# Three fused layers on one core: u's transfers grouped on the SP queue, the next y split in two portions, output products ahead of h2's last

## The chip, the cores and the metric

The kernel runs on one core of one Trainium2 chip. TensorE (PE) multiplies matrices, VectorE (DVE), ScalarE (ACT) and GpSimd (POOL) work element by element, SyncE's queue (SP) and ScalarE's issue DMA transfers. Each engine works through its own list in order, and semaphores hold an instruction until what it needs is there. The metric is the device time of the whole program in microseconds; lower is better.

## The reference

Three layers follow each other. The decay attention is linear, the next layer is `h - tanh(h)` between two products, the last a SoLU layer with a layer norm.

```python
for t in range(S):                    # S=768, 4 x 8 heads of 64
    state = gamma * state + einsum('bhd,bhe->bhde', k[:, :, t], v[:, :, t])
    y[:, :, t] = scale * einsum('bhd,bhde->bhe', q[:, :, t], state)
x = y.transpose(0, 2, 1, 3).reshape(3072, 512)
h = x @ w_in                          # 512 -> 2048
y = (h - tanh(h)) @ w_out             # 2048 -> 512
h2 = y @ w_in2                        # 512 -> 1024
sm = exp(h2 - max(h2)); sm = sm / (sum(sm) + 1e-9)
solu = h2 * sm
ln = (solu - mean(solu)) / sqrt(var(solu) + 1e-6) * g_ln
out = ln @ w_out2                     # 1024 -> 512
```

## The kernel before

Every factor of a product is held as two float32 parts, high and low (`xh`, `xl`), and a product is three matmuls: high by high, high by low, low by high. A matmul here is 128x128 weights against a 128x512 tile. The parts are made by a ScalarE cast (the high part) and a subtraction on VectorE or GpSimd (the low part).

The first product of the second layer, and h2 of the third, are done for a pair of token tiles together with seven products in place of eight (P1 to P7), whose operands are parts of y as they are (`yha`, `yla`, for P1, P2, P4) and sums of such parts (`ysum`, split into `yhs`, `yls`, for P5, P6, P7, P3). In a pair's h2 each product is six matmuls (L922), 42 in all. Some products are added up in a PSUM bank, others are copied by ScalarE (`keep2`, L929, tiles `part`) and added by VectorE (`add_half`, L937), which also takes the minimum of the negated row (`nm`). P6 continues in the bank of P1 and may start only when P1's copy has been taken; P7 continues P6's.

The 3072 tokens are 24 tiles, 12 pairs. The PE order of the last stage is written out by hand (`tc.manual_schedule`); the order on the other engines and on SP comes from a scheduler, which `pin` (`tc.keep_in_program_order`) binds to program order. Pair j's stage, `pair_of`, runs P1, P2, P6, P5, P7, P4, P3; behind it come the output products of pair j-1, `outs`, the odd tile and then the even one, each 24 matmuls into `po` (L986). Pair 0 lies inside the last slab of the layer before, whose steps f run from 0 to 15.

A tile of h2 becomes `u` in `soft`: exponential (L947, ACT), multiply with row sum (L949, DVE), subtract the mean (L951, ACT), sum of squares (L953, ACT), a 32x32 transposition (L955, DVE), then a store to DRAM, `ud` (L956, SP). `turn` loads it back with the token and feature axes exchanged (L969, SP), first the pair's odd tile, then its even one. `trans` splits it into `uh` (L160, ACT) and `ul` (L161, DVE). P4 finishes the odd tile, P3 the even one. `split_y` (L498 on ACT, L475 on POOL) and `sum_y` (L482 to L485, POOL) prepare y of later pairs; `load_y` (L468, SP) loads it. The store of y is L388, its copies out of PSUM are L385 (DVE) and L387 (ACT).

Of the kernel before, what the change touches and what calls it, by code (L numbers as in the profile page):

```python
# [26 lines left out]
F32 = mybir.dt.float32  # L27
F32R = mybir.dt.float32r
I32 = mybir.dt.int32
AF = mybir.ActivationFunctionType  # L30
ALU = mybir.AluOpType
# [5 lines left out]
P = 128  # L37
DM = H * D
# [7 lines left out]
NF1, NF2, NK = FF1 // P, FF2 // P, DM // P  # L46
# [42 lines left out]
def body(ctx: ExitStack, tc, z, w_in, w_out, w_in2, w_out2, g_ln, cst, tab, out):  # L89
    nc = tc.nc  # L90
# [8 lines left out]
    def pin(ins, on=True):  # L99

        if on:
            tc.keep_in_program_order(ins)

    def t4(shape, dtype, name):
        return big.tile(shape, dtype, tag="t4", name=name)

    def t2(shape, dtype, name):
        return mid.tile(shape, dtype, tag="t2", name=name)
# [10 lines left out]
    ud = [yd.tile([P, NF2 * P], F32, name=f"ud{i}") for i in range(NTT)]  # L119
# [37 lines left out]
    P1, P2, P6, P5, P7, P4, P3 = range(7)  # L157

    def parts(h, o, src, eng):
        nc.scalar.copy(h, src)  # L160
        eng.tensor_tensor(o, src, h.bitcast(F32), ALU.subtract)  # L161
# [297 lines left out]
    yl, ys, ysum = {}, {}, {}  # L459
# [11 lines left out]
    def on_pool(n, out, a, b, op):  # L471
        k = out.shape[1] // n
        for i in range(n):
            at = slice(i * k, (i + 1) * k)
            nc.gpsimd.tensor_tensor(out[:, at], a[:, at], b[:, at], op)  # L475

    def sum_y(j):
        t = yl[j]
        a11, a12, a21, a22 = (t[:, i, k : k + 2, :] for i in range(2) for k in (0, 2))
        s = ysum[j] = t4([P, 4, 2, P], F32, "ysum")  # L480
        s1, s2, s3, s4 = (s[:, i, :, :] for i in range(4))
        nc.gpsimd.tensor_tensor(s1, a21, a22, ALU.add)  # L482
        nc.gpsimd.tensor_tensor(s2, s1, a11, ALU.subtract)
        nc.gpsimd.tensor_tensor(s3, a11, a21, ALU.subtract)
        nc.gpsimd.tensor_tensor(s4, a12, s2, ALU.subtract)  # L485

    def split_y(j):
        t, s = yl.pop(j), ysum.pop(j)
        a22 = t[:, 1, 2:4, :]
        ya, ys_ = ([t4([P, 4, 2, P], F32R, f"y{n}{g}") for n in "hl"] for g in "as")  # L490
        flat = "p a k t -> p (a k t)"
        for to, lo, n, src in (
            (ya, 0, 2, t[:, 0, :, :].rearrange("p k t -> p (k t)")),
            (ya, 2, 1, a22.rearrange("p k t -> p (k t)")),
            (ys_, 0, 4, s.rearrange(flat)),
        ):
            h, o = (w[:, lo : lo + n, :, :].rearrange(flat) for w in to)
            nc.scalar.copy(h, src)  # L498
            on_pool(n, o, src, h.bitcast(F32), ALU.subtract)
        at = {P1: (ya, 0), P2: (ya, 1), P4: (ya, 2)}  # L500
        at |= {P5: (ys_, 0), P6: (ys_, 1), P7: (ys_, 2), P3: (ys_, 3)}
        ys[j] = {m: [w[:, i, :, :] for w in to] for m, (to, i) in at.items()}


    wl, xs, sums = {}, {}, {}
# [157 lines left out]
    for n in range(NF1):  # L663
# [8 lines left out]
        k = 2 * B + n - LATER  # L672
# [7 lines left out]
        else:  # L680

            dec1.n = 2 * NF1
            m = n - (NF1 - 4)
# [148 lines left out]
    for n in range(len(q) + 1):  # L832
        now, was = n < len(q), n > 0
        p, j = q[n] if now else (NSB, 0)
        todo = list(per[j]) if p == 1 else []
# [70 lines left out]

    w2p = ctx.enter_context(tc.tile_pool(name="w2p", bufs=7))
    sp = ctx.enter_context(tc.tile_pool(name="sp", bufs=3))
    uc, ut, sc2 = {}, {}, {}

    def bank2():
        pool, tag = bank_of[0]
# [29 lines left out]
    def soft(i, h, last):  # L942

        hn, nmx = h[0], h[1][last]
        ex = t4([P, FF2], F32, "ex")
        ssum = sp.tile([P, 1], F32, tag="ssum", name="ssum")
        nc.scalar.activation(ex, hn, AF.Exp, bias=nmx, scale=-1.0, accum_out=ssum)  # L947
        us = sp.tile([P, 1], F32, tag="us", name="us")
        nc.vector.scalar_tensor_tensor(ex, hn, 1.0, ex, ALU.mult, ALU.mult, accum_out=us)  # L949
        nc.vector.tensor_scalar(us, us, -1.0 / FF2, None, ALU.mult)  # L950
        nc.scalar.activation(hn, ex, AF.Identity, bias=us)  # L951
        ssq = sp.tile([P, 1], F32, tag="ssq", name="ssq")
        nc.scalar.activation(ex, ex, AF.Square, bias=us, accum_out=ssq)  # L953

        nc.vector.transpose(ex, hn)  # L955
        nc.sync.dma_start(out=ud[i], in_=ex)  # L956

        nc.vector.tensor_scalar(ssum, ssum, 1e-9, -1.0, ALU.add, ALU.mult)
        nc.vector.reciprocal(ssum, ssum)
        nc.vector.tensor_scalar(ssq, ssq, ssum, ssum, ALU.mult, ALU.mult)  # L960
        nc.vector.tensor_scalar(ssq, ssq, 1.0 / FF2, 1e-6, ALU.mult, ALU.add)
        sc = sp.tile([P, 1], F32, tag="sc", name="sc")
        nc.gpsimd.tensor_tensor(sc, ssq, mhalf, ALU.pow)
        nc.gpsimd.tensor_tensor(sc, sc, ssum, ALU.mult)
        uc[i], sc2[i] = hn, sc

    def turn(j):
        for i in (2 * j + 1, 2 * j):
            nc.sync.dma_start(  # L969
                out=uc[i].rearrange("p (c i b) -> p c i b", c=NF2, i=B),  # L970
                in_=ud[i].rearrange("(i a) (g c b) -> (a g) c i b", i=B, g=4, c=NF2),
            )

    def trans(i):
        u = uc.pop(i)
        uh, ul = (t4([P, NF2 * P], F32R, "u" + n) for n in "hl")
        parts(uh, ul, u, nc.vector)
        ut[i] = [w.rearrange("p (f t) -> p f t", f=NF2) for w in (uh, ul)]

    def outp(i):  # L980
        uh, ul = ut.pop(i)
        po = ps_o.tile([P, DM], F32, tag="o", name="po")
        for f in range(NF2):
            bh, bl = dec2.w[f]
            for n, (a, b) in enumerate(((uh, bh), (uh, bl), (ul, bh))):
                nc.tensor.matmul(  # L986
                    po, a[:, f, :], b, start=f == 0 and n == 0, stop=f == NF2 - 1 and n == 2
                )
        ob = t2([P, DM], F32, "ob")
        nc.scalar.activation(ob, po, AF.Copy, scale=sc2.pop(i))  # L990
        at = i % B * S + i // B * P
        nc.scalar.dma_start(out=out[at : at + P, :], in_=ob)
# [42 lines left out]
    for n, (s, f) in enumerate(steps):  # L1035
        if n:
            if f == 0:
                y_banks(s)
                if s == NSB - 1:
                    bank_of[:] = [(ps_a, "r"), (ps_a, "r"), (ps_h, "h"), (ps_h, "h")]  # L1040
            load_g(n + 5)
            load_wo(n + 4)
            if n + 2 < len(steps):
                split_p(n + 2)
            if n + 2 < NF1:
                split_wo(n + 2)
            products_y(f, gp.pop(n), wo[f], py)
        if f == NF1 - 1:
            keep_y(s, py)
        if s >= NSB - 3 and n % 2 == 0 and com.n[2] < 12:  # L1050
            com.step()
        m = n - 2 * NF1 - 6
        if m >= 0 and m % 3 == 0:
            step2(m // 3)
        if s == NSB - 1:
            if f == 0:
                load_y(0)
            if f == 2:
                sum_y(0)
                load_y(1)  # L1060
            if f == 5:
                split_y(0)
            if f == 9:
                sum_y(1)
                load_y(2)
            if f == 8:
                pair = Pair(0)
            for m in {8: (P1, P2), 9: (P6,), 10: (P5,), 11: (P7,), 12: (P4,), 13: (P3,)}.get(f, ()):
                pair.part(m)
            if f == 12:  # L1070
                split_y(1)
            if f == 13:
                turn(0)
            if f == 14:
                sum_y(2)
    G.close()
    M.close()

# [2 lines left out]
    ps_o = ctx.enter_context(tc.tile_pool(name="ps_o", bufs=2, space=PSUM, reuse_waits="tile"))  # L1081
    NJ = NTT // 2
# [3 lines left out]
    def pair_of(j, before):  # L1086
        pair = Pair(j)
        for n, m in enumerate((P1, P2, P6, P5, P7, P4, P3)):
            if n == 0 and j + 1 < NJ:
                split_y(j + 1)  # L1090
            if n == 2 and j + 2 < NJ:
                sum_y(j + 2)
            if n == 4 and j + 3 < NJ:
                load_y(j + 3)
            if n == 5 and before is not None:
                trans(2 * before + 1)
            pair.part(m)
        turn(j)
        if before is not None:
            trans(2 * before)  # L1100

    def outs(j, after=None):
        for half in (1, 0):
            outp(2 * j + half)
            if after is not None:
                trans(2 * after + half)

    with tc.manual_schedule(engines={mybir.EngineType.PE}):
        for j in range(1, NJ - 1):
            pair_of(j, j - 1)  # L1110
            if j < NJ - 2:
                outs(j - 1)
        pair_of(NJ - 1, None)
        outs(NJ - 3, NJ - 2)
        outs(NJ - 2, NJ - 1)
        outs(NJ - 1)


# [57 lines left out]
```

## Time and profile before

| | |
|---|---|
| median of 3 runs | 867.75 us (866.66 to 869.57) |
| profiled execution | 867.15 us, span 865.4 us |
| mean granted clock of PE | 0.986 of full speed |
| PE busy | 829.4 us, 96% of the span |
| PE weight load | 675.4 us, 78% |
| DVE busy | 540.7 us, 62% |
| ACT busy | 461.2 us, 53% |
| POOL busy | 291.6 us, 34% |
| last stage, pairs 1 to 11 | from 606.9 us to the span's end |

All in microseconds from the span's start. Busy times of engines overlap, so they don't add up. PE's busy share is near the whole, so the profile is read for the places where PE waits, and for the clock that was granted to it there. In a timeline, a row is a run of like instructions with its start and length; the square bracket is the idle time before it and what ended that.

### The profile page before, as it was taken

The page shows a single profiled execution, that of the slowest core. Times are in us where ns is not written, and L with a number is a line of the kernel's source. Part 1 is how long each engine was busy: PE and PEld are TensorE (multiplying, and loading weights), DVE is VectorE, ACT ScalarE, POOL GpSimd, SP SyncE. Part 2 cuts the span into 40 slices and gives each one's busy share as a digit, 9 for nine tenths or more (in the row PEclk, how much of TensorE's full clock was granted, in tenths as well). Part 3 has the DMA queues.
Part 4 walks back from the last instruction along what each step waited for, and adds up shares of the span by engine and source line. Part 5 has one row for each costly group of instructions (what it writes and reads, how often), then busy time and mean ns, then how long its engine had stood idle before and what let it go on. Part 6 is the DMA issues. An engine that isn't in the chain of part 4 may idle for free.

```text
span 865.4 us, 16366 instructions
## 1 busy us (share of the span) xinstructions
PE 829.4 (96%) x6296; PEld 675.4 (78%) x6296; DVE 540.7 (62%) x999; ACT 461.2 (53%) x868; POOL 291.6 (34%) x304
## 2 busy tenths in 40 slices
PE   5799999999999899999999999999899999999898
PEld 4678888788877687888788888888577777777786
DVE  3788975999858757223573979473555455555561
ACT  4655744646555546444462627244566666666662
POOL 4411100180634348433300350142544444444210
PEclk9899999999999899999999999999899999999999
DMA  9658654344899626955584647440766666665574
GB/s 361 254 215 301 254 190 156 120 147 177 303 362 335 236 82 223 411 198 174 195 337 127 226 121 281 148 169 25 171 145 147 147 147 145 146 147 122 121 162 105
DMA packets 168460, 169.41 MB, mean 196 GB/s; under 512 B 105664, under 2 KB 117952, under 8 KB 168384
## 3 DMA queue, kind: packets, MB, share of 16 engines
q1 hardware_dynamic: 160032, 153.38, 57.1%
q10 hardware_dynamic: 8352, 15.00, 4.7%
q8 instruction: 49, 0.80, 0.4%
q14 instruction: 27, 0.22, 0.1%
HBM read 107.02 MB, written 61.34 MB: 195 GB/s over the span
## 4 chain that ended last, share of the span: by engine, by line
PE 81%; DVE 5%; DMA 4%; ACT 3%; issue 3%; POOL 2%; SPq 0%; ACTq 0%; POOLq 0%; DVEq 0%
PE py L377 29%; PE ph L750 15%; PE po L986 14%; PE ph L922 11%; PE ph L352 8%; PE out L228 2%; DMA hn<-ud 2%; PE sc L228 2%; DMA z<-z 1%; DMA raw<-w_in 1%; ACT part L929 1%; POOL hs L768 1%; DVE hn L937 1%; POOL yls L475 1%; ACT uh L160 0%
## 5 line engine op out<-in xcount | busy, mean ns | idle before, releaser
L377 PE MATMUL py<-gp,w 128*128 128x512 f32 x768 | 175.4, 389 | 0.0
L377 PEld LDWEIGHTS py<-gp,w 128*128 128x128 f32 x768 | 144.1, 188 | 29.9
L986 PE MATMUL po<-w,uh 128*128 128x512 f32 x384 | 118.6, 390 | 0.0
L768 POOL TENSOR_TENSOR hs<-hs,th 128x512 f32<-128x512 f32 x48 | 66.8, 1395 | 95.8 <-ACT th L766 91.1
L986 PEld LDWEIGHTS po<-w,uh 128*128 128x128 f32 x384 | 72.1, 188 | 14.8
L352 PE MATMUL ph<-xh,w 128*128 128x512 f32 x256 | 82.1, 395 | 0.8 <-DVE w L154 0.8
L377 PE MATMUL py<-gh,w 128*128 128x512 f32 x256 | 79.2, 390 | 0.3 <-ACT gh L365 0.3
L986 PE MATMUL po<-w,ul 128*128 128x512 f32 x192 | 76.4, 398 | 0.6 <-DVE us L950 0.6
L153 ACT CAST w<-wf 128x512 fp32r<-128x512 f32 x70 | 43.1, 621 | 57.6 <-DVE wf L144 47.1
L922 PE MATMUL ph<-w,yhs 128*128 128x512 f32 x192 | 63.9, 416 | 6.4 <-ACT part L929 5.8
L475 POOL TENSOR_TENSOR yla<-yl,yha 128x256 fp32r<-128x256 f32 x36 | 26.3, 756 | 127.2 <-ACT yha L498 127.2
L766 ACT ACTIVATE th<-hs 128x512 f32<-128x512 f32 x48 | 30.3, 631 | 60.4 <-DVE hs L776 52.4
L937 DVE CUSTOM_DVE_ANT_0 hn<-ph,part 128x512 f32<-128x512 f32 x24 | 16.6, 691 | 72.5 <-ACT part L929 54.9
L154 DVE TENSOR_TENSOR w<-wf,w 128x512 fp32r<-128x512 f32 x70 | 51.2, 736 | 15.3 <-ACT w L153 14.5
L161 DVE TENSOR_TENSOR gp<-g,gp 128x512 fp32r<-128x512 f32 x64 | 48.4, 770 | 18.8 <-ACT gp L160 18.6
L750 PE MATMUL ph<-xh,wch 128*128 128x512 f32 x140 | 57.3, 409 | 1.6 <-DVE hs L776 1.6
L352 PEld LDWEIGHTS ph<-xh,w 128*128 128x128 f32 x256 | 48.0, 188 | 11.8 <-DVE w L154 1.3
L377 PEld LDWEIGHTS py<-gh,w 128*128 128x128 f32 x256 | 48.0, 188 | 10.6 <-ACT gh L365 0.7
L929 ACT COPY part<-ph 128x512 f32<-128x512 f32 x36 | 21.1, 586 | 64.7 <-PE ph L922 64.7
L750 PE MATMUL ph<-xh,wcl 128*128 128x512 f32 x140 | 55.4, 396 | 0.0
L750 PE MATMUL ph<-xl,wch 128*128 128x512 f32 x140 | 55.3, 395 | 0.0
L776 DVE TENSOR_TENSOR hs<-ph,part 128x512 f32<-128x512 f32 x48 | 32.9, 686 | 35.2 <-PE ph L750 20.8
(123 smaller groups left out, 1811.9 us busy)
## 6 DMA issues: line engine op xcount, KB each, us to landing
z<-z SPq DMA_DIRECT2D x48, 512.0 KB, 6.4
g<-gd SPq DMA_DIRECT2D x64, 256.0 KB, 5.3
raw<-w_in SPq DMA_DIRECT2D x24, 512.0 KB, 6.3
raw<-w_out SPq DMA_DIRECT2D x24, 512.0 KB, 4.4
gd<-hs SPq DMA_DIRECT2D x48, 256.0 KB, 3.9
ud<-ex SPq DMA_DIRECT2D x24, 512.0 KB, 4.5
hn<-ud SPq DMA_DIRECT2D x24, 512.0 KB, 5.8
y1d<-ysb SPq DMA_DIRECT2D x24, 256.0 KB, 3.9
```

The source lines that it names most:

```text
L153: pin(nc.scalar.copy(hi, wf), fixed)
L154: pin(eng.tensor_tensor(lo, wf, hi.bitcast(F32), ALU.subtract), fixed)
L161: eng.tensor_tensor(o, src, h.bitcast(F32), ALU.subtract)
L228: pin(nc.tensor.matmul(o, a, b, start=True, stop=True, skip_group_check=True), held[0])
L352: nc.tensor.matmul(ph, a[:, k, :], x, start=n == 0, stop=n == 3 * NK - 1), s < 2
L377: nc.tensor.matmul(py[e], a[:, cols], x, start=f == 0 and n == 0, stop=f == NF1 - 1 and n == 2)
L475: nc.gpsimd.tensor_tensor(out[:, at], a[:, at], b[:, at], op)
L750: nc.tensor.matmul(ph, a, x, start=first and n == 0, stop=n == 5, skip_group_check=True)
L768: eng.tensor_tensor(g, h, th, ALU.subtract)
L776: nc.vector.tensor_tensor(h, ph, part, ALU.add)
L922: nc.tensor.matmul(ph, x[:, r, :], w, start=first and n == 0, stop=n == 5, skip_group_check=True)
L986: nc.tensor.matmul(po, a[:, f, :], b, start=f == 0 and n == 0, stop=f == NF2 - 1 and n == 2)
```

## The change

Three things change, all in or near the last stage.

First, the store of `u` and its load are pinned, so on SP a pair's two stores come first and then its two loads.

Second, `split_y` can do one half: the direct parts (`yha`, `yla`) or the sums' parts (`yhs`, `yls`). In a pair, the direct half of the next pair's y is split after P1 and the sums' half after P6; the sums of the pair after that are taken after P7. In the last slab, `split_y(0)` moves from f=5 to f=4, `sum_y(1)` from 9 to 6, `split_y(1)` from 12 to 9, `sum_y(2)` from 14 to 11.

Third, the first three output products of the odd tile of the pair before (two with `uh`, one with `ul`) stand between P4 and P3 of pairs 1 to 10; the other 21 follow P3 as before.

```diff
-    def split_y(j):
+    def split_y(j, halves=(0, 1)):
...
+        for g in halves:
+            y = [t4([P, 4, 2, P], F32R, f"y{n}{'as'[g]}") for n in "hl"]
+            if g:
+                todo = ((0, 4, ysum.pop(j).rearrange(flat)),)
+                at = {P5: 0, P6: 1, P7: 2, P3: 3}
+            else:
+                t = yl[j]
+                todo = (
+                    (0, 2, t[:, 0, :, :].rearrange("p k t -> p (k t)")),
+                    (2, 1, t[:, 1, 2:4, :].rearrange("p k t -> p (k t)")),
+                )
+                at = {P1: 0, P2: 1, P4: 2}
+            for lo, n, src in todo:
+                h, o = (w[:, lo : lo + n, :, :].rearrange(flat) for w in y)
+                nc.scalar.copy(h, src)
+                on_pool(n, o, src, h.bitcast(F32), ALU.subtract)
...
-        nc.sync.dma_start(out=ud[i], in_=ex)
+        pin(nc.sync.dma_start(out=ud[i], in_=ex))
...
-            nc.sync.dma_start(
+            pin(nc.sync.dma_start(
...
-    def outp(i):
-        uh, ul = ut.pop(i)
-        po = ps_o.tile([P, DM], F32, tag="o", name="po")
-        for f in range(NF2):
+    def outp(i, fs):
+        uh, ul = ut[i]
+        if fs[0] == 0:
+            po_of[i] = ps_o.tile([P, DM], F32, tag="o", name="po")
+        po = po_of[i]
+        for f in fs:
...
-            if f == 5:
+            if f == 4:
                 split_y(0)
+            if f == 6:
+                sum_y(1)
             if f == 9:
-                sum_y(1)
                 load_y(2)
...
-            if f == 12:
+            if f == 9:
                 split_y(1)
+            if f == 11:
+                sum_y(2)
             if f == 13:
                 turn(0)
-            if f == 14:
-                sum_y(2)
...
         for n, m in enumerate((P1, P2, P6, P5, P7, P4, P3)):
-            if n == 0 and j + 1 < NJ:
-                split_y(j + 1)
-            if n == 2 and j + 2 < NJ:
+            if n == 5 and before is not None:
+                trans(2 * before + 1)
+            if m == P3 and before is not None:
+                outp(2 * before + 1, range(1))
+            pair.part(m)
+            if n in (0, 2) and j + 1 < NJ:
+                split_y(j + 1, (n // 2,))
+            if n == 4 and j + 2 < NJ:
                 sum_y(j + 2)
             if n == 4 and j + 3 < NJ:
                 load_y(j + 3)
-            if n == 5 and before is not None:
-                trans(2 * before + 1)
-            pair.part(m)
```

PE, from P4 of a steady pair (bank `ph2_7576`) to the second group of output products; P3 is what goes on in the bank of P5 and reads `yhs`, `yls`; `uh_7572` and `ul_7573` are the odd tile of the pair before. Before:

```order
L922 MATMUL ph2_7576<-w_6212,yha_7325 128x512 x2
L922 MATMUL ph2_7576<-w_6212,yla_7326 128x512
L922 MATMUL ph2_7554<-w_6069,yhs_7327 128x512 x2
L922 MATMUL ph2_7554<-w_6069,yls_7328 128x512
L922 MATMUL ph2_7554<-w_6249,yhs_7327 128x512 x2
L922 MATMUL ph2_7554<-w_6249,yls_7328 128x512
L986 MATMUL po_7633<-w2_6325,uh_7572 128x512 x2
L986 MATMUL po_7633<-w2_6325,ul_7573 128x512
L986 MATMUL po_7633<-w2_6388,uh_7572 128x512 x2
```

and changed (the lines of the file have shifted by 3 to 8):

```order
L925 MATMUL ph2_7576<-w_6212,yha_7334 128x512 x2
L925 MATMUL ph2_7576<-w_6212,yla_7335 128x512
L991 MATMUL po_7602<-w2_6325,uh_7572 128x512 x2
L991 MATMUL po_7602<-w2_6325,ul_7573 128x512
L925 MATMUL ph2_7549<-w_6069,yhs_7357 128x512 x2
L925 MATMUL ph2_7549<-w_6069,yls_7358 128x512
L925 MATMUL ph2_7549<-w_6249,yhs_7357 128x512 x2
L925 MATMUL ph2_7549<-w_6249,yls_7358 128x512
L991 MATMUL po_7602<-w2_6388,uh_7572 128x512 x2
```

The group of `w2_6325`, with its `ul` product, has moved ahead of P3's six products.

VectorE at the same place: `hn_7504` is the odd tile of this pair's h2 (its first row adds P7's `part`, the third takes P4's bank `ph2_7576`), `hn_7507` the even tile, which P3 finishes. Before:

```order
L937 ISA hn_7504,nm_7506<-ph2_7554,part_7569 128x512
L937 ISA nm_7506 128x1
L937 ISA hn_7504,nm_7505<-ph2_7576,part_7569,nm_7506 128x512
L937 ISA nm_7505 128x1
L161 TENSOR_TENSOR ul_7573<-hn_7319,uh_7572 128x1024
L937 ISA hn_7507,nm_7509<-ph2_7554,part_7552,nm_7508 128x512
```

and changed:

```order
L940 ISA hn_7504,nm_7506<-ph2_7549,part_7562 128x512
L940 ISA nm_7506 128x1
L940 ISA hn_7504,nm_7505<-ph2_7576,part_7562,nm_7506 128x512
L940 ISA nm_7505 128x1
L161 TENSOR_TENSOR ul_7573<-hn_7319,uh_7572 128x1024
L952 SCALAR_TENSOR_TENSOR ex_7584,us_7587<-hn_7504,ex_7584 128x1024
```

The subtraction that makes `ul_7573` stands behind the add of P4's bank in both; the multiply of the odd tile now comes ahead of the even tile's last add.

ScalarE around the beginning of pair 1: `ysb` are the copies of the last y, `hn` in L951 (changed: L954) and `ex` in L953 (changed: L956) belong to pair 0's tiles, `part` is the copy after P1. Before:

```order
L387 COPY ysb_6924<-py_6467 128x512
L387 COPY ysb_6930<-py_6469 128x512
L951 ACTIVATE hn_6684<-ex_6871,us_6874 128x1024
L953 ACTIVATE ex_6871,ssq_6878<-ex_6871,us_6874 128x1024
L498 CAST yhs_6957<-ysum_6907 128x1024
L929 COPY part_6976<-ph2_6969 128x512
```

and changed:

```order
L387 COPY ysb_6924<-py_6467 128x512
L954 ACTIVATE hn_6689<-ex_6876,us_6879 128x1024
L387 COPY ysb_6930<-py_6469 128x512
L956 ACTIVATE ex_6876,ssq_6883<-ex_6876,us_6879 128x1024
L932 COPY part_6962<-ph2_6955 128x512
L503 CAST yhs_6987<-ysum_6808 128x1024
```

The cast of the sums has moved behind the part copy, and one pass over the even tile has moved between the two copies of y.

## Rows read from the trace of the kernel before

**Rows 1.** Chain of waits, 634 to 656 us: start, length, what.
```profile
634.73 6.82 PE ph L922 x30
...
641.56 0.60 ACT part L929
...
642.18 0.69 DVE hn L937
...
642.94 1.66 PE ph L922 x6
```

**Rows 2.** Window of a steady pair: length, busy (count) by engine, PEclk, DMA, GB/s.
```profile
644.60:665.57 20.97, 20.92 (x91) 16.74 (x91) 11.01 (x27) 13.64 (x21) 9.23 (x15) 1.00 0.66 150
```

**Rows 3.** Timeline of PE, pair 1: start, length, work, idle before and releaser.
```profile
606.93 0.73 PE L922 MATMUL ph<-w,yha 128*128 128x512 f32 x2 [0.52 <-ACT ysb L387]
...
613.35 1.22 PE L922 MATMUL ph<-w,yhs 128*128 128x512 f32 x2 [3.41 <-ACT part L929]
...
620.27 0.62 PE L922 MATMUL ph<-w,yha 128*128 128x512 f32 x2
```

**Rows 4.** Timeline of ACT, pair 1.
```profile
611.77 1.04 ACT L498 CAST yhs<-ysum 128x1024 fp32r<-128x1024 f32 x1 [2.28 <-POOL ysum L485]
```

**Rows 5.** Timeline of ACT and PE, pair 11.
```profile
817.92 1.04 ACT L160 CAST uh<-hn 128x1024 fp32r<-128x1024 f32 x1 [1.16 <-DMA hn<-ud]
...
819.50 0.72 PE L922 MATMUL ph<-w,yhs 128*128 128x512 f32 x2 [2.35 <-ACT part L929]
...
823.95 0.39 PE L922 MATMUL ph<-w,yhs 128*128 128x512 f32 x1
```

**Rows 6.** Timeline of PE, an even tile's first `ul` product.
```profile
778.17 0.50 PE L986 MATMUL po<-w,ul 128*128 128x512 f32 x1 [0.41 <-DVE us L950]
```

**Rows 7.** Timeline of PE, pair 2.
```profile
634.56 0.62 PE L922 MATMUL ph<-w,yha 128*128 128x512 f32 x2
...
641.36 0.62 PE L922 MATMUL ph<-w,yha 128*128 128x512 f32 x2
...
644.98 0.50 PE L986 MATMUL po<-w,ul 128*128 128x512 f32 x1
645.32 0.62 PE L986 MATMUL po<-w,uh 128*128 128x512 f32 x2
```

**Rows 8.** Timeline of DVE, pair 2.
```profile
643.03 0.75 DVE L937 CUSTOM_DVE_ANT_0 hn<-ph,part,nm 128x512 f32<-128x512 f32 x1
...
643.70 1.22 DVE L161 TENSOR_TENSOR ul<-hn,uh 128x1024 fp32r<-128x1024 f32 x1
```

**Rows 9.** Timeline of ACT, pair 2.
```profile
642.04 1.05 ACT L160 CAST uh<-hn 128x1024 fp32r<-128x1024 f32 x1
```

**Rows 10.** Groups by line, 623 to 812 us: busy, mean ns, idle before.
```profile
L949 DVE SCALAR_TENSOR_TENSOR ex<-hn,ex 128x1024 f32<-128x1024 f32 x18 | 22.0, 1223 | 0.0
...
L947 ACT ACTIVATE ex<-hn,nm 128x1024 f32<-128x1024 f32 x18 | 20.8, 1154 | 12.3 <-DVE nm L937 12.3
```

**Rows 11.** Timeline of SP: a store of pair 0, an even load.
```profile
608.94 0.59 SPq L956 DMA_DIRECT2D ud<-ex  x1
...
662.55 0.59 SPq L969 DMA_DIRECT2D hn<-ud  x1
```

**Rows 12.** DMA issues on the page: count, size, median us from issue to landing.
```profile
ud<-ex SPq DMA_DIRECT2D x24, 512.0 KB, 4.5
hn<-ud SPq DMA_DIRECT2D x24, 512.0 KB, 5.8
```

**Rows 13.** Timelines of DVE and POOL: like subtractions, alone and beside GpSimd's.
```profile
594.08 0.69 DVE L161 TENSOR_TENSOR gp<-g,gp 128x512 fp32r<-128x512 f32 x1
...
602.18 1.89 POOL L475 TENSOR_TENSOR yls<-ysum,yhs 128x256 fp32r<-128x256 f32 x2
...
602.33 1.15 DVE L161 TENSOR_TENSOR gp<-g,gp 128x512 fp32r<-128x512 f32 x1 [0.56 <-ACT gp L160]
```

**Rows 14.** Window with a long PE wait in the second layer; columns as in rows 2.
```profile
335.50:339.00 3.50, 1.87 (x9) 1.49 (x9) 3.50 (x4) 0.63 (x1) 3.23 (x2) 1.00 1.02 381
```

## What was predicted

> **What bounds the kernel now.** I read the last stage first, since every edit lies there, and began with the chain of waits over one pair [rows 1]: it is TensorE nearly throughout, broken only by a ScalarE copy and a VectorE add after P7. The window from one pair's first output product to the next pair's [rows 2] says the same: 20.97 us, of which PE is busy 20.92. A pair issues 42 h2 and 48 output products. By the chain, 30 products take 6.82 us, so one goes out every 0.2273 us and ninety need 20.46. A steady pair therefore loses only about 0.5 us. The page's PE share, 96%, is an average; what can be won here is the sum of a few gaps, and what can be lost is any new gap on PE.
>
> The timelines show four gaps. I call them A to D.
> - A, start of pair 1 [rows 3, 4]: P1 waits 0.52 for ScalarE's copy of the last y, and P6 waits 3.41 because ScalarE's part copy stands behind the `yhs` cast at 611.77, which waited 2.28 for GpSimd's sums. Then the 18 products from 613.35 to 620.27 take 6.92 in place of 4.09: 2.8 more, at the lower of the clock's two levels (2.4 and 1.2 GHz).
> - B, every pair: P3 waits for VectorE's first add, then the first `ul` product waits for VectorE. Together this is the 0.5 us above.
> - C, pair 11 [rows 5]: P6 waits 2.35 for a part copy behind the `uh` cast at 817.92, which waited 1.16 for a load. The 12 products from 819.50 to 823.95 take 4.45 in place of 2.73: 1.72 more, in the same way.
> - D, even tiles: the first `ul` product waits for VectorE in six pairs, each 0.06 to 0.70 by the products' issue times, 1.8 together; the row of the worst is [rows 6].
>
> **The change part by part.** I count from the issue of P4's first product in pair 2, 641.36, as zero [rows 7]. No instruction's work changes; only places do.
>
> *Three output products before P3.* Before, P4 goes out from 0 to 1.36, P3 to about 3.0 (six products of 0.227, after a wait of 0.22), two `uh` products at 3.07, the `ul` product at 3.62 (644.98), and the next at 3.96 (645.32). The `ul` product waits for VectorE's subtraction, which runs 643.70 to 644.92, that is +2.34 to +3.56 [rows 8]. It comes there because ScalarE casts `uh` from 642.04 to 643.09 [rows 9], behind the part copy, and VectorE does the a1 add, then the a0 add of P4's result (643.03 to 643.78), then the subtraction. The order of VectorE and ScalarE there is the same in both programs. The a0 add must wait for P4, which has not moved, so `ul` is still ready at +3.56. What ran under that wait was P3, 1.36 us. Now P3 stands behind the `ul` product: PE issues P4 to 1.36, waits some 0.4 for `uh`, issues two products, waits some 1.4 for `ul`, issues it at +3.62, and only at +3.96 comes to P3, which ends at +5.32. Before, all these products were out at +3.96. The cost is P3's whole 1.36 us. Pairs 2 to 10 do this: 9 x 1.36 = +12.2. The gap B is in that: the stall for the a1 add goes, the wait for `ul` swallows it.
>
> *The even tile and the SP order (D).* After P3 come 21 odd products (4.77), so the even tile starts at +10.1 and its `ul` is needed at +10.5. P3's last add ends near 6.3 (0.75 long [rows 8]); the exponential of 1.15 and the cast of 1.05 behind it end near 8.7, the multiply of 1.22 near 8.9, the subtraction of 1.22 near 10.2 [rows 8 to 10]. So 0.3 us are spare, if the load has come. Before, the even load went out at 662.55, +21.2, behind the even store [rows 11]; now both stores go first, and I estimate the even load at +20, when the even store, issued near +14.7, has landed (4.5) and SP has come back. With 5.8 for the load [rows 12] it is there at +26, and the pair lasts 22.3, so it comes 4 us into the next pair, well before the cast at 7.7. The odd load now leaves near +15 in place of +13.7, lands at +21, and is needed at +23. D's 1.8 us go: -1.8. If the 0.3 us spare are not there, each pair pays what is missing; that is in the rivals.
>
> The Trainium skill, SBUF — State Buffer, section "SBUF: two separate sides", says that VectorE (with two inputs in SBUF) and GpSimd (reading SBUF) exclude each other from a shared port pair, and the second to come is blocked for the whole instruction. The trace agrees in kind [rows 13]: a 128x512 subtraction on VectorE took 0.69 alone and 1.15 beside GpSimd's. By that rule the even subtraction would be late whenever GpSimd's `yla` chain began ahead of it; the price is among the rivals.
>
> *The two portions of y (A).* `ysum` of pair 1 is now summed at step f=6 and cast after P6, so P6 no longer waits for GpSimd: 3.4 and the clock's part go. But two things are late in their place. ScalarE's order now has one 128x1024 pass (L954, 1.15 like [rows 10]) between the two copies of y, so P1 starts near 608.05 and not 606.93. And pair 1 too has the three products before P3: their `uh` needs tile 1's load. The store left at 608.94 [rows 11] and can now leave up to 0.8 earlier, since two of y's stores stand ahead of it on SP and not three; it lands 4.5 later, the load takes 5.8 [rows 12], the cast 1.05: `uh` at 619.5 to 620.3. PE, from 608.05 with 36 products (8.18), is through P4 at 616.2 and waits 3.3 to 4.1. From `uh` at 619.5 the `ul` is ready 1.25 later (the subtraction), at 620.8; one `ul` product, P3, 21 odd products and 24 even ones take 0.2 + 1.4 + 4.8 + 5.5, and the even `ul`, whose load comes after the odd one, costs perhaps 0.5: pair 1 ends near 633.2 at full clock. Before, it ended at 634.56, where pair 2's P1 begins [rows 7]. Stalls of 2.35 and 3.41 were followed by the lower clock [rows 3, 5]; I add C's 1.72 and get 634.9, a net +0.3; between -1.4 (no lower clock) and +1.8.
>
> *End (C).* ScalarE's order before pair 11 now has the even cast, the odd square, then the part copy of P1, and that cast waits for the exponential after P3 of pair 10, not for a load. The cast ends at 8.7, square and copy take 1.5 more: P6 at +10.25, where PE, with P1 and P2 (2.73) after +5.32, is ready at +8.05: 2.2 in place of 2.35, with another 0.2 at P7, and the same clock. Net +0.1. If all of C went it would be -4.1 (2.35 and 1.72).
>
> *Steps moved in the last slab.* GpSimd and ScalarE have gaps there and PE does not wait for them in the profile; 0, from -0.3 to +0.5.
>
> Sum: +12.2 - 1.8 + 0.3 + 0.1 = +10.8. The profiled execution took 867.15 (span 865.4), the median of three 867.75: 878.0 against the first, 878.6 by the second. I say 878.
>
> **The rivals.**
> 1. *ScalarE's part copies come free (not slower).* If the copies of pairs 1 and 11 no longer stand behind a cast that waits, A's whole 0.5 + 3.4 + 2.8 (waits and clock) and C's 4.1 go: about -10.8, with D -12.6, against +12.2: 866.8. The point from which it decides is a cost per pair of 1.40; under it the kernel is faster. For it: the y sums are early now. Against: the order puts L954 ahead of the second y copy, pair 1's new products wait for a load that lands near 618.5, and the cast ahead of pair 11's copy waits for P3. 8%.
> 2. *The clock falls in each pair.* The new waits, 0.4 and 1.4, have two products between them. A stretch of 3.50 us in which PE was busy 1.87, its idle time in one piece of 1.6, kept a granted clock of 1.00 [rows 14]; a wait of 2.35 was followed by the lower level [rows 5]. If each pair falls, 9 x 1.72 more: 893.5; if a third do, 883. 12%.
> 3. *The even tile is late.* GpSimd's `yla` subtractions now follow P1 and begin just after VectorE's even subtraction. Beside one, VectorE's subtraction took 1.15 in place of 0.69 [rows 13]; two of GpSimd's took 1.89, 0.95 each. One that goes first costs 0.95 less the spare 0.3, 0.65 in nine pairs, +5.9: 884; in half of them, 881. Against: the `yla` cast stands behind two ScalarE passes that come with or after the even tile's own cast. 12%.
> 4. *PE's wait is hidden*, because `ul` is ready at P4's end. Then B's 0.5 go too in ten pairs, with D: about 860. It needs the subtraction ahead of the a0 add, and the order has it behind. 3%.
>
> **How the numbers follow.** My own case has 65%: 878, with 874 to 881 for the terms of A and C and a tenth per pair either way. The range 871 to 888 takes in rival 3, the milder form of rival 2 and most of C's gain; it leaves out rivals 1 and 4 and the full form of 2. About 0.3% (2.6 us) is what a measurement of this kernel can tell. Faster by more: rival 4 and a little of 1, 0.05; within: the rest of 1, 0.06; slower: 0.89.
>
> **What would show it.** Right: in a pair of the changed kernel, two `uh` products after P4, then a wait of about 1.4 for VectorE at the `ul` product, P3 1.36 later than its old place, a period near 22.3; no wait at an even tile's `ul`; no wait for a part copy at pair 1's P6, but one of 2.5 to 4 after its P4. Wrong: a period under 21.3, a granted clock under 1.00 inside pairs 2 to 10, or VectorE's subtraction ahead of the a0 add.

## The result and the profile after

| | before | changed |
|---|---|---|
| median, the runs of one chip | 867.2 us (864.3 to 869.57, 4 runs) | 877.41 us (877.04 to 879.79, 4 runs) |
| ratio to before | | 1.0125, 95% interval 1.0089 to 1.0161 |
| profiled execution, span | 867.15, 865.4 us | 877.57, 875.7 us |
| PE busy | 829.4 us, 96% | 827.2 us, 94% |

The change made the kernel slower by 1.25%, 10.2 us between the medians and 10.3 between the spans. PE's busy time did not grow; its waiting did.

The timeline of PE in pair 2 answers to [rows 7]; P4 begins at 642.65. The columns are start, length, work, idle time before it and what ended that.

```profile
642.65 0.62 PE L925 MATMUL ph<-w,yha 128*128 128x512 f32 x2
...
644.43 0.73 PE L991 MATMUL po<-w,uh 128*128 128x512 f32 x2 [0.26 <-ACT uh L160]
646.27 0.50 PE L991 MATMUL po<-w,ul 128*128 128x512 f32 x1 [1.10 <-DVE ul L161]
646.60 0.62 PE L925 MATMUL ph<-w,yhs 128*128 128x512 f32 x2
```

The `ul` product goes out 3.62 after P4's first product, and the next thing 3.95 after it: just as before. But that next thing is now P3. VectorE in the same pair, answering to [rows 8]:

```profile
644.32 0.75 DVE L940 CUSTOM_DVE_ANT_0 hn<-ph,part,nm 128x512 f32<-128x512 f32 x1
...
644.99 1.22 DVE L161 TENSOR_TENSOR ul<-hn,uh 128x1024 fp32r<-128x1024 f32 x1
```

The subtraction runs from +2.34 to +3.56 after P4's first product, to the hundredth where it was. The groups by line from 623 to 812 us, in which eight pairs' early products lie, show what that sums to (busy, mean ns, idle before and releaser):

```profile
L991 PE MATMUL po<-w,uh 128*128 128x512 f32 x279 | 87.4, 394 | 2.1 <-ACT uh L160 2.1
L991 PE MATMUL po<-w,ul 128*128 128x512 f32 x139 | 55.3, 398 | 9.0 <-DVE ul L161 8.8 <-DVE ssq L964 0.3
```

Windows of the changed kernel, with the columns of [rows 2]: a steady pair, the stretch behind pair 1's wait, and pair 11's first products.

```profile
642.64:664.98 22.34, 20.98 (x91) 16.73 (x90) 11.13 (x26) 13.74 (x20) 9.13 (x16) 1.00 0.59 134
620.00:624.40 4.40, 4.35 (x9) 2.98 (x10) 2.64 (x6) 2.26 (x3) 0.00 (x0) 0.50 0.95 169
829.00:834.50 5.50, 3.48 (x15) 2.31 (x13) 4.98 (x12) 5.39 (x8) 0.74 (x2) 1.00 0.17 71
```

A pair lasts 22.34 in place of 20.97, at a granted clock of 1.00. The second window is at the lower level, the third is not. PE at the beginnings of pairs 1, 2 and 11 (answering to [rows 3, 5, 7]):

```profile
607.65 0.73 PE L925 MATMUL ph<-w,yha 128*128 128x512 f32 x2 [1.45 <-ACT ysb L387]
...
620.01 1.22 PE L991 MATMUL po<-w,uh 128*128 128x512 f32 x2 [3.90 <-ACT uh L160]
...
635.85 0.62 PE L925 MATMUL ph<-w,yha 128*128 128x512 f32 x2
...
831.58 0.73 PE L925 MATMUL ph<-w,yhs 128*128 128x512 f32 x2 [2.02 <-ACT part L932]
```

Pair 1's P6 waits for no copy any more; the 3.90 after its P4 stands in that place. The pair starts 0.72 later and ends 1.29 later than before (635.85 against 634.56): term A is +1.29. From there to pair 11's first product are 190.83 against 179.70 us, +11.13, of which 0.68 are three products that were issued behind it before: pairs 2 to 10 cost +10.45. From pair 11 to the end the kernel gains 2.12, less those 0.68: -1.44. Together 10.3, the difference of the spans.

SP's two stores and two loads of pair 2, now in that order (compare [rows 11]), and then the landing times of all loads of u in this kernel:

```profile
654.05 3.66 SPq L959 DMA_DIRECT2D ud<-ex  x2
658.88 4.26 SPq L972 DMA_DIRECT2D hn<-ud  x2
```

```profile
DMA to landing us min/median/max: 6.2/7.2/9.1
```

The odd load leaves at +16.2, and the median load takes 7.2 where [rows 12] had 5.8; both will matter below.

### The profile page after: what moved, and what is told of

Same layout as the page of the kernel before. It is cut to its first block, busy times and chain, and to the rows that moved or that the text cites. A ratio compares the mean times of both kernels' runs of the same rounds, so it can differ in the third digit from the quotient of the medians.

```text
span 875.7 us, 16359 instructions
## 1 busy us (share of the span) xinstructions
PE 827.2 (94%) x6296; PEld 674.0 (77%) x6296; DVE 542.4 (62%) x999; ACT 463.2 (53%) x868; POOL 291.3 (33%) x304
## 4 chain that ended last, share of the span: by engine, by line
PE 78%; DMA 7%; DVE 6%; issue 4%; ACT 4%; POOL 1%; SPq 0%; ACTq 0%; DVEq 0%; POOLq 0%
PE py L377 28%; PE ph L753 15%; PE po L991 12%; PE ph L925 9%; PE ph L352 9%; DMA hn<-ud 2%; PE out L228 2%; PE sc L228 2%; DMA raw<-w_in 1%; DVE ul L161 1%; DMA z<-z 1%; DVE hn L940 1%; DMA wcd<-wch 1%; DMA ud<-ex 1%; ACT part L932 1%
## 5 line engine op out<-in xcount | busy, mean ns | idle before, releaser
L991 PE MATMUL po<-w,uh 128*128 128x512 f32 x384 | 120.4, 395 | 6.3 <-ACT uh L160 6.3
L991 PEld LDWEIGHTS po<-w,uh 128*128 128x128 f32 x384 | 71.9, 189 | 24.9 <-ACT uh L160 10.5
L991 PE MATMUL po<-w,ul 128*128 128x512 f32 x192 | 76.6, 399 | 10.4 <-DVE ul L161 10.1
L475 POOL TENSOR_TENSOR yla<-yl,yha 128x256 fp32r<-128x256 f32 x36 | 28.6, 822 | 105.0 <-ACT yha L503 90.6
L925 PE MATMUL ph<-w,yhs 128*128 128x512 f32 x192 | 60.5, 397 | 2.1 <-ACT part L932 2.0
L160 ACT CAST gp<-g 128x512 fp32r<-128x512 f32 x64 | 38.7, 619 | 29.8 <-DMA g<-gd 17.7
```

The source lines that it names most:

```text
L925: nc.tensor.matmul(ph, x[:, r, :], w, start=first and n == 0, stop=n == 5, skip_group_check=True)
L991: nc.tensor.matmul(po, a[:, f, :], b, start=f == 0 and n == 0, stop=f == NF2 - 1 and n == 2)
```

## The experiments

The theory was that P3 is the work that ran while VectorE made `ul`, and that the early products put it behind that wait. Ratios are to the kernel before on the same chip, with 95% intervals.

**The change without its early products.** Its edit:

```diff
-            if m == P3 and before is not None:
-                outp(2 * before + 1, range(1))
...
-                outs(j - 1, 1)
+                outs(j - 1, 0)
```

> The changed kernel with all 24 output products of the odd tile behind P3 again; stores and loads pinned and y in two portions as changed. Theory (P3 was the work that ran while VectorE made ul, and the early products put it behind that wait): the wait of 1.38 before an ul product goes from every pair, the period falls from 22.33 to 20.9 or 21.0, pair 1 still waits about 2.7 for the odd tile's load: 877.4 - 12.2 - 1.4 = 863.8. Rival (the stores-first order or the split casts made the odd tile's ul late, whatever stands in front): the period stays above 22 and the time near 877.

Measured 861.49 us, ratio 0.9931 (0.9910 to 0.9952): 16 us below the changed kernel, and faster than before. Pair 3 on PE:

```profile
664.28 0.73 PE L925 MATMUL ph<-w,yhs 128*128 128x512 f32 x2
...
665.77 0.61 PE L991 MATMUL po<-w,uh 128*128 128x512 f32 x2
666.32 0.50 PE L991 MATMUL po<-w,ul 128*128 128x512 f32 x1
666.66 0.62 PE L991 MATMUL po<-w,uh 128*128 128x512 f32 x2
```

P4's first product was at 662.71, so `ul` goes out at +3.61 once more, with P3 in front of it. The theory holds. The time is 2 us below the 863.8 that was expected; in the trace pair 1 takes 25.85 in place of the changed kernel's 28.20, where 1.4 less was expected, and from pair 11 on, like for like, it is 0.5 less.

**The early products alone**, on the kernel before:

```diff
+            if m == P3 and before is not None:
+                outp(2 * before + 1, range(1))
             pair.part(m)
```

> The kernel before with one thing changed: the first three output products of the odd tile between P4 and P3. Theory: 1.36 in each of ten pairs, +13.6, and the waits of the even tiles' ul (1.8) go because that tile starts 1.36 later: 867.2 + 13.6 - 1.8 = 879. Rival (the loss needs the changed SP order or the two portions): 867 to 870.

Measured 878.0 us, ratio 1.0129 (1.0100 to 1.0159). One pair:

```profile
666.64 0.73 PE L988 MATMUL po<-w,uh 128*128 128x512 f32 x2 [0.26 <-ACT uh L160]
668.47 0.50 PE L988 MATMUL po<-w,ul 128*128 128x512 f32 x1 [1.10 <-DVE ul L161]
668.81 0.62 PE L922 MATMUL ph<-w,yhs 128*128 128x512 f32 x2
```

These are the same waits, without the SP order or the two portions. The early products carry the whole loss, and on top of them the other two parts change nothing that can be told (1.0125 against 1.0129). No even tile waits at its `ul` from pair 2 to pair 10 here either: for that the SP order was not needed.

**The pinned stores and loads alone.**

```diff
-        nc.sync.dma_start(out=ud[i], in_=ex)
+        pin(nc.sync.dma_start(out=ud[i], in_=ex))
...
-            nc.sync.dma_start(
+            pin(nc.sync.dma_start(
```

> The kernel before with the stores and loads of u pinned, nothing else. Theory: only the even tiles' waits can go, -1.8, and the odd load leaves about 1.4 later than before, at +15, in a period of 20.97: it lands at about +21 to +22, the cast wants it at +21.7, so up to 0.5 a pair may come back: 865.4 to 870. Rival (stores first is a gain by itself, as both loads are sooner): 863 or less.

Measured 868.29 us, ratio 0.9993 (0.9977 to 1.0009): no change. Most even waits went and odd ones came, as the trace of ScalarE and of PE shows; pairs 2 to 10 took 182.4 us in place of 179.7. In this execution pair 1 made up for it, with 25.26 in place of 27.63:

```profile
664.42 1.05 ACT L160 CAST uh<-hn 128x1024 fp32r<-128x1024 f32 x1 [0.97 <-DMA hn<-ud]
```

```profile
615.59 0.73 PE L922 MATMUL ph<-w,yhs 128*128 128x512 f32 x2 [3.40 <-ACT part L929]
...
666.78 0.49 PE L986 MATMUL po<-w,ul 128*128 128x512 f32 x1 [0.43 <-DVE ul L161]
```

The first row of PE is P6 of pair 1. It waits 3.40, as before (3.41, [rows 3]), but the granted clock behind it, from 615.59 to 620.50, is 1.00, where before it was 0.50 from 613.4 to 617.

**The two portions alone**, by taking the pins off the first experiment:

```diff
-        pin(nc.sync.dma_start(out=ud[i], in_=ex))
+        nc.sync.dma_start(out=ud[i], in_=ex)
...
-            pin(nc.sync.dma_start(
+            nc.sync.dma_start(
```

> The kernel before with y split in two portions and the sums moved earlier in the last slab, nothing else. Theory: pair 1's P6 no longer waits 3.4 for a part copy; P1 starts later by about 0.7, and the odd tile's uh is then waited for some 2 to 3 with the lower clock behind it: net -1 to -4 there, the end as in the changed kernel (about -1.5): 862 to 866. Rival (the whole of gap A and the end's gap go): 857 or less.

Measured 867.23 us, ratio 0.9986 (0.9968 to 1.0004): no change that can be told, and 1 us above the range given. Pair 1's wait is down to 1.15, but even tiles still wait, and pair 11 as before:

```profile
775.22 0.50 PE L991 MATMUL po<-w,ul 128*128 128x512 f32 x1 [0.52 <-DVE us L953]
...
816.45 0.73 PE L925 MATMUL ph<-w,yhs 128*128 128x512 f32 x2 [2.36 <-ACT part L932]
```

Neither part gives anything alone; the two together (first experiment) give 0.7%. One reason can be read: with pins alone ScalarE's `yhs` cast (1.04) still runs between the two tiles' passes, so the second store is late, and the odd load, now behind it on SP, left at +16.3; with both parts that cast comes later, and the load left at +14.0.

**The subtraction ahead of the add.** VectorE's order was the second claim.

```diff
-        parts(uh, ul, u, nc.vector)
+        nc.scalar.copy(uh, u)
+        pin(nc.vector.tensor_tensor(ul, u, uh.bitcast(F32), ALU.subtract), i % 2 == 1)
...
-        nc.vector.tensor_tensor_reduce(
+        pin(nc.vector.tensor_tensor_reduce(
...
-        )
+        ), seen == 1)
```

> The changed kernel with one order held on VectorE: the odd tile's ul subtraction ahead of the add of P4's result. Theory (the early ul product waits because that add, which waits for P4, stands ahead of the subtraction): ul is ready about 0.55 earlier, after the cast of uh and 1.22, and PE's wait falls from 1.38 to about 0.8 in nine pairs and pair 1: 877.4 - 5.3 = 872. Rival (the wait is for the odd tile's load or for the cast, so the order on VectorE is nothing): 877.

Measured 879.61 us, ratio 1.0131 (1.0100 to 1.0162): not 872. The idle time before `ul` did fall, from 1.10 to 0.5 or 0.6, as expected, but one for `uh` grew in front of it, 0.4 to 1.8 from pair to pair. The worst pair, on PE, ScalarE and VectorE:

```profile
691.33 1.12 PE L992 MATMUL po<-w,uh 128*128 128x512 f32 x2 [1.81 <-ACT uh L980]
```

```profile
690.23 1.04 ACT L980 CAST uh<-hn 128x1024 fp32r<-128x1024 f32 x1 [1.44 <-DMA hn<-ud]
```

```profile
691.31 1.23 DVE L981 TENSOR_TENSOR ul<-hn,uh 128x1024 fp32r<-128x1024 f32 x1 [1.79 <-ACT uh L980]
692.45 0.75 DVE L940 CUSTOM_DVE_ANT_0 hn<-ph,part,nm 128x512 f32<-128x512 f32 x1
```

The load is late, the add behind the subtraction is late with it, and that add begins the chain to the next store and load. In this pair the clock fell too: behind the wait of 1.81 the granted clock was 0.52 from 691.33 to 694.40, and the pair lasted 24.40 where the others lasted 21.9 to 22.5. So rival 2 of the prediction, which the changed kernel doesn't show, came in one pair of this one. A new theory followed: the odd load closes a loop of one pair, and the pinned order makes that loop long.

**Two `uh` products ahead of P3, `ul` behind it.**

```diff
-                outp(2 * before + 1, range(1))
+                outp(2 * before + 1, range(1), (0, 1))
...
+                if f or n in ns:
+                    nc.tensor.matmul(
```

> The changed kernel with only the two uh products of the early group ahead of P3 and their ul product behind it. Theory: P3 again runs while VectorE makes ul; PE loses 0.42 for uh and nothing or 0.1 at ul, the period is 20.9 to 21.0, so 877.4 - 12.2 to 12.6, and pair 1 gains about 1.4 more: 863.5. Rival (any output product ahead of P3 costs what P3 takes): 875 or more.

Measured 872.89 us, ratio 1.0055 (1.0036 to 1.0074): between the two expectations. PE at the place in question:

```profile
730.36 0.72 PE L992 MATMUL po<-w,uh 128*128 128x512 f32 x2 [0.26 <-ACT uh L160]
730.93 0.63 PE L925 MATMUL ph<-w,yhs 128*128 128x512 f32 x2
...
732.32 0.40 PE L992 MATMUL po<-w,ul 128*128 128x512 f32 x1
...
738.97 0.50 PE L992 MATMUL po<-w,ul 128*128 128x512 f32 x1 [0.59 <-DVE ul L161]
```

The wait for the odd `ul` is gone, as the theory has it. The last row is the even tile's, a new wait: the scheduler, given this PE order, put ScalarE's L954 pass ahead of the even cast, which was late by that 1.14:

```profile
735.52 1.14 ACT L954 ACTIVATE hn<-ex,us 128x1024 f32<-128x1024 f32 x1
736.57 1.03 ACT L160 CAST uh<-hn 128x1024 fp32r<-128x1024 f32 x1
```

A pair still lasts 22.3. So this run doesn't weigh the two alone.

**An early split**, so that the three products are ready when P4 ends:

```diff
-            if n == 5 and before is not None:
+            if n == 4 and before is not None:
                 trans(2 * before + 1)
...
-        nc.scalar.copy(t, ph)
+        pin(nc.scalar.copy(t, ph), held)
```

with `held` for P6's and P7's copies, and the odd tile's cast and subtraction and the adds of P7 and P4 pinned likewise.

> The changed kernel, all three early products kept, with the odd tile's cast held between ScalarE's copies of P6 and P7 and its subtraction ahead of VectorE's add for P7. Theory: by the trace of the kernel without early products the odd load lands 0.9 to 1.5 before P4's first product, so uh and ul are ready when P4 ends; the three products then cover the add, PE loses 0.1 to 0.3 a pair in place of 1.93, pair 1 stays as in the changed kernel: 877.4 - 9 x 1.7 = 862. Rival (the load lands too late and its cast now holds the copy of P7, so P3 waits as long as ul did): 875 or more.

Measured 879.24 us, ratio 1.0137 (1.0107 to 1.0167): the rival was right. ScalarE and VectorE in pair 3:

```profile
667.25 1.04 ACT L980 CAST uh<-hn 128x1024 fp32r<-128x1024 f32 x1 [3.12 <-DMA hn<-ud]
668.21 0.58 ACT L932 COPY part<-ph 128x512 f32<-128x512 f32 x1
```

```profile
668.33 1.23 DVE L981 TENSOR_TENSOR ul<-hn,uh 128x1024 fp32r<-128x1024 f32 x1 [5.35 <-ACT uh L980]
669.47 0.68 DVE L940 CUSTOM_DVE_ANT_0 hn<-ph,part 128x512 f32<-128x512 f32 x1
670.31 0.75 DVE L940 CUSTOM_DVE_ANT_0 hn<-ph,part,nm 128x512 f32<-128x512 f32 x1
```

Copy, subtraction and both adds stand behind one load.

**The same from pair 2 on.**

```diff
-            if n == 4 and before is not None:
+            if before is not None and n == (4 if before else 5):
...
-            if m == P3 and before is not None:
+            if m == P3 and before:
```

> The same, but pair 1, whose odd load comes last, without early products and with the split behind P7's copy as before. Theory: 862 of that kernel less about 3 in pair 1 (wait before P3 and part of the lower clock): 858 to 859. Rival (the load late in each pair): 873 or more; rival (pair 1 is worth nothing here): 862.

Measured 879.31 us, ratio 1.0128 (1.0098 to 1.0157): the first rival, no gain over the run before. Pair 1's wait fell to 2.30 and the pair by 1.9 us; pairs 2 to 10 took 1.1 more, with `uh` waited for 0.4 to 1.7 in each of them. In this run and the one before it pair 4 lasts 25.0 and 24.9, again at the lower level of the clock (0.50 from 692 to 694 and from 694 to 696).

**Loads not pinned**, on the run with the subtraction ahead (the edit takes `pin` off the store and the load, as above).

> The kernel with ul ahead of the add (879.6), but stores and loads not pinned: store odd, load odd, store even, load even. Theory (with both loads together each takes 7.2 and the odd one now comes last to PE: late uh, late add, late store, late load of the next pair, a loop of one pair): the odd load lands 1.5 sooner, uh is waited for 0.3 again and ul 0.5 to 0.6, so 872 as first expected of that run. Rival (the loop is not the load's): 877 to 880.

Measured 873.75 us, ratio 1.0077 (1.0050 to 1.0104). From pair 2 on `uh` is waited for 0.27 in each pair, where it was 0.4 to 1.8:

```profile
708.22 0.73 PE L992 MATMUL po<-w,uh 128*128 128x512 f32 x2 [0.27 <-ACT uh L980]
709.66 0.50 PE L992 MATMUL po<-w,ul 128*128 128x512 f32 x1 [0.71 <-DVE ul L981]
```

So it was the load. Against the run with the pins, pairs 2 to 10 take 4.0 less, of which 2.4 lie in the one pair whose clock had fallen, and pair 1 takes 2.1 less, its wait for `uh` 1.88 in place of 3.94.

**Loads not pinned, with the early split from pair 2** (the same edit on that kernel).

> The kernel with the odd tile split before P7's copy and no early products in pair 1 (879.3), but stores and loads not pinned. Theory: the loop through the odd load is 1.5 shorter, so uh is late by less in each pair and after some pairs not at all; 860 if it catches up, 872 if it stays at the loop's length. Rival (early cast is bad because it holds P7's copy back, whatever the load does): 877 or more.

Measured 868.85 us, ratio 1.0013 (0.9994 to 1.0031), 10 us less than with the pins. Pairs 2 and 3, by their first early product:

```profile
643.73 0.73 PE L992 MATMUL po<-w,uh 128*128 128x512 f32 x2 [1.01 <-ACT uh L980]
...
665.47 0.61 PE L992 MATMUL po<-w,uh 128*128 128x512 f32 x2
```

The wait for `uh` is gone from pair 3 on; the loop catches up as expected. The time of 860 did not come: P3 now goes out 0.61 after the `ul` product and not 0.34, behind VectorE's add, which is behind the subtraction, and four pairs still wait 0.5 to 0.9 at `ul`.

**Three products that are ready.** On the kernel without early products, the last group of an even tile moves between P4 and P3. In pair j it is that of pair j-2's tile, whose parts have long been ready:

```diff
+            if m == P3 and before:
+                outp(2 * before - 2, range(NF2 - 1, NF2))
...
-                outs(j - 1, 0)
+                outs(j - 1, 0, None, 1)
```

> The kernel without early products (861.5) with three other output products between P4 and P3: the last group of the even tile of the pair before that, whose uh and ul were ready long ago; nothing is computed twice, that tile's end moves. Theory (it is not the place that costs but the waiting for ul there): the three cover the 0.2 to 0.3 that P3 waits for VectorE's first add and P3 then covers ul; the period falls from about 20.9 to 20.4 or 20.5: 861.5 - 4.5 = 857. Rival (three products between P4 and P3 cost P3's time wherever they come from): 873 or more.

Measured 859.18 us, ratio 0.9901 (0.9872 to 0.9930). Pair 2:

```profile
638.64 0.62 PE L925 MATMUL ph<-w,yha 128*128 128x512 f32 x2
...
639.32 0.62 PE L991 MATMUL po<-w,uh 128*128 128x512 f32 x2
639.78 0.39 PE L991 MATMUL po<-w,ul 128*128 128x512 f32 x1
640.00 0.62 PE L925 MATMUL ph<-w,yhs 128*128 128x512 f32 x2
...
641.36 0.62 PE L991 MATMUL po<-w,uh 128*128 128x512 f32 x2
641.82 0.39 PE L991 MATMUL po<-w,ul 128*128 128x512 f32 x1
```

There is no gap left: from P4's first product at 637.96 to the next pair's at 658.36 are 20.40 us, ninety products at 0.2267. Of pairs 2 to 9 only pair 4 lasts longer, 20.82. In pairs 2 to 10 it is the same place and the same number of products as in the changed kernel, at 20.40 us a pair against 22.34: what costs is whose data they wait for. Pair 1 has no early products here, so the 18 us between the two medians are not all of that. Against the kernel without early products the intervals overlap; there the gain is shown by the trace, 198.7 against 203.5 us from pair 1's first product to pair 11's for the same products.

**The same, and pair 11 filled.**

```diff
+            if before is None and n in (2, 4):
+                outp(2 * j - 3, range(2) if n == 2 else range(2, 3))
```

> The same, and in pair 11 nine output products of tile 19 that are ready, six ahead of P6 and three ahead of P7, where PE waits 1.2 and 1.0 for ScalarE's copies. Theory: these waits are covered: 2 less than the run without them, 855. Rival (the copies stand behind a chain that only comes later): the same time as without them.

Measured 856.7 us, ratio 0.9882 (0.9855 to 0.9910), the lowest median here. Its P6 and P7 wait for no copy any more:

```profile
813.95 0.62 PE L925 MATMUL ph<-w,yhs 128*128 128x512 f32 x2
...
817.49 0.72 PE L925 MATMUL ph<-w,yhs 128*128 128x512 f32 x2
```

The two intervals overlap, so whether it beats the run without can't be told from the times. In the traces, from pair 1's first product to PE's last, it takes 242.6 us against 243.6: half of the 2 that were expected, and a wait of 0.53 for a `ul` has come at 843.36.

## Why the prediction was right, and where not

- *The pair's cost* was the forecast's largest term and came out as worked out: the period 22.34 for 22.3, `ul` at +3.62, P3 at +3.95. With the even tiles, pairs 2 to 10 gave +10.45 against +12.2 - 1.8 = +10.4. The kernel without early products takes 177.68 us for pairs 2 to 10, which parts the two: +12.5 for the early products, -2.0 for the even tiles. The runs with and without the early products show the cause.
- *D*, the even tiles: no wait for `ul` there from pair 2 to pair 10; right, though the early products do that without the SP order too.
- *A* was mis-sized: +0.3 forecast, +1.29 measured. `uh` came at 620.0, inside the 619.5 to 620.3, but I took the early end of it; the wait was 3.90. And I took 1.72 for the clock: the twelve products from 621.27 to 626.18 took 4.91 in place of 2.73, 2.2 more.
- *C* had the wrong sign: +0.1 forecast, -1.44 measured. The wait for the copy was as worked out (2.02 for 2.2); the step that failed is "the same clock". In this execution the granted clock stayed at 1.00 behind 2.02, where before it had been at the lower level behind 2.35. The forecast took the clock from the length of the wait, and the runs don't bear that out: behind 3.40 it was 1.00 (pins alone), behind 1.81 it was 0.52 (the subtraction ahead).
- A was 1.0 too low and C 1.5 too high, and they nearly cancelled. That is luck, and both clock terms are read from one execution each; what the forecast had right is the +10.4 of pairs 2 to 10, where the clock was 1.00.
- *The odd load's margin* failed too, almost without a cost here (waits for `uh` of 0.26 to 0.30). I had it leave near +15, land at +21 and be needed at +23. It left at +16.2 and took 6.2 at the least: +22.4 or later, against a cast at +23.0. That was why the subtraction's order alone won nothing, as the run with the loads not pinned shows.
- *Rival 1* did not occur: pair 1's P6 waits for no copy, but 3.90 stand behind its P4, and pair 11's copy is still waited for; only the clock's part of C went. *Rival 2* did not occur: the waits of 0.26 and 1.10 left the clock at 1.00. *Rival 3*: in pairs 2 to 10 ScalarE's order kept GpSimd's chain behind the even subtraction (in pair 2 from 652.95, the subtraction from 651.53 to 652.75). In pair 1 the two met, GpSimd's recorded from 629.43 and the subtraction from 629.45; there the subtraction took its 1.21 and GpSimd's three took 3.22 in place of 2.14, so the price that I put on VectorE fell on GpSimd. *Rival 4* did not occur; the early split with unpinned loads comes nearest to it, and doesn't reach it.

Left open: in the profiled executions pair 1 begins anywhere from 606.05 to 611.09 us; these two are of the two kernels with ready products, whose work is the same up to pair 11. Differences of a few us between spans are therefore read by stage; the cause is open. That the pins and the portions together give 0.7% and neither alone is measured; how much of it is the odd load's earlier issue and how much pair 11 is not separated.

## What to carry to other kernels

Before an instruction is moved ahead, ask what ran under the wait it brings along: an instruction that must wait takes everything behind it on an in-order engine into its wait, and the work it overtakes was the cover. To fill a gap, take work whose inputs have long been there, even if it comes from further back. And where a result returns to its own engine through a store and a load, work out the loop's length before anything in it is tightened: what is late in one turn is late in the next. A cost of the clock that was read behind one wait of one execution belongs in the range of a forecast and not in its sum.

## What the runs showed of the hardware

Loads of u took longer where both stores stood ahead of both loads on SP. In the nine kernels with that order (the changed one, and those without early products, with pins alone, with the subtraction ahead, with `uh` ahead, the two with the early split and pins, and the two with ready products) the median from issue to landing was 6.9 to 7.5 us; in the five where a store came between the loads, the kernel before among them, 5.6 to 5.8. The two kernels with the subtraction ahead differ in that order alone: 7.5 and 5.7. What in the transfers takes the time was not looked at.

The granted clock after one wait of PE: 1.00 after 2.02 (pair 11, changed), 0.50 after 3.90 (pair 1, changed). The length of that one wait doesn't settle it: at the same place in pair 1 it was 0.50 after 3.41 (before) and after 3.40 (early products alone), but 1.00 after 3.40 (pins alone), and it was 0.52 after 1.81 (pair 4, the subtraction ahead). What does settle it is open.

A VectorE and a GpSimd subtraction that met made one of the two longer: in pair 1 of the changed kernel GpSimd's three 128x256 ones took 3.22 in place of 2.14 beside VectorE's, which kept its 1.21; in [rows 13] it was VectorE's that took 1.15 in place of 0.69. Spans on GpSimd are rough.
